# Sliding-window attention and a token-mixing MLP on one core: some transposes of x made by DMA, the mixing products with 128 columns, and a new table of emission

## The chip, the cores and the metric

The kernel runs on one core of one Trainium2 chip. The metric is the device time of one execution in microseconds (us), lower being better. A core has TensorE (PE, with its weight loads as PEld), VectorE (DVE), ScalarE (ACT), GpSimd (POOL) and SyncE (SP). Here POOL and SP only issue DMAs: POOL all loads, SP all stores.

## The reference

There are 8 batches, 8 heads, 576 tokens, and 64 channels in a head.

```python
scores = q @ k.T / 8 + slope[h] * -(i - j)      # only 0 <= i - j < 128, else -1e9
attn   = softmax(scores);  x = attn @ v          # x: (8, 576, 512), heads side by side
wq = x @ w_q;  wk = x @ w_k                      # (8, 576, 64)
mixed  = (wq @ wk.T / 8) @ x                     # token mixing; no softmax here
out    = relu(mixed) @ w_out                     # (8, 576, 512), float32
```

Because nothing stands between the two products of the mixing, the kernel computes `g = wk.T @ x` (64 x 512) first and then `mixed.T = g.T @ wq.T`.

## The kernel before, in words

All work of a batch `b` is cut into steps, each made by `plan.op(name, ...)` and belonging to one engine:

- **Loads** (POOL): q, k and v of the batch, cast to fp16 on the way (`ldsix`, `ldqk`, `ldqkt`, `ldv...`; line 234).
- **q and k transposes** (PE, then a copy by ACT or DVE out of PSUM): `tsix`, `tqk`, `tqkt` and their copies `etsix`, `etqk`, `etqkt`.
- **Scores** `sc` (line 483), exponential `exp` on ACT (L496), multiplication by the table of biases `mul` on DVE (L500). A batch has two halves `z` of two pairs of heads, and three pieces `u` in a half.
- **Values**: per pair of heads `hp` the matmuls `pva` (128-row stationary) and `pvd` (64x64 stationary), both L526; then `nrm` on DVE (L554, L555), which divides by the sums and writes x of this pair, tokens on partitions.
- **x transposed**: `xt` on PE (five transposes of 128x128, L572) into PSUM, and `ext`, a copy of 576 columns by ACT (L222) or DVE (L224) into `xT`.
- **Mixing**: `wk` (L608) and its copy `ewk`; `wq` (L637) and `ewq`; `g` (L650), whose copy into `gm` is three steps `eg` (r = None: all partitions, columns 0 to 255; r = 0 and r = 1: the halves exchanged, columns 256 to 511); then four steps `mx` (j = 0 to 3, L673), each followed by `emx`, which applies the relu and writes `rm`.
- **Output**: nine tiles of 128 tokens per pair of batches, `po` (four matmuls, L703), copy `eo`, store `st` on SP (L710).

The order of all steps is written out in the table `ORDER`. An entry is the step's number, the letter of its engine (P, A, D, G for POOL, S), for PE the PSUM bank, and `+n` for n extra matmuls on zeros (L721, `keep`) ahead of it. Each engine executes its own steps in the order of the table; semaphores between engines follow from the data and from PSUM banks. So a step whose input is late holds up everything behind it on its engine.

A mixing step uses the PE array in a tile shape: `xt`, `tqk`, `wk`, `po`, `pva` use the whole 128x128; `sc`, `pvd`, `mx` 64x64; `wq`, `g`, `tsix` 128 (or 96) rows by 64 columns.

The last PE steps of the table, from the mixing of batch 4 on (an argument is the batch, then the pair of heads, the column j, the first token of the tile, or half and piece):

```
wk(4) pvd(5,3) tqk(6,c1,x1) g(4) wq(4) xt(5,3) mx(4,j1) mx(4,j3) mx(4,j0) wk(5) tqk(6,c1,x0) mx(4,j2) g(5) sc(6,z0u1)
sc(6,z1u0) sc(6,z0u0) po(4,o384) sc(6,z0u2) po(4,o128) sc(6,z1u1) sc(6,z1u2) wq(5) tqk(7,c0,x1) po(4,o256) pva(6,1)
pva(6,0) mx(5,j0) pvd(6,1) tqk(7,c1,x1) pvd(6,0) mx(5,j1) po(4,o0) tqk(7,c0,x0) pva(6,2) mx(5,j2) pvd(6,2) mx(5,j3)
xt(6,0) tqk(7,c1,x0) pva(6,3) xt(6,2) pvd(6,3) sc(7,z0u1) sc(7,z0u0) po(5,o640) xt(6,3) po(5,o768) sc(7,z1u2)
sc(7,z0u2) po(5,o512) pva(7,0) xt(6,1) pvd(7,0) sc(7,z1u1) sc(7,z1u0) wk(6) xt(7,0) wq(6) pva(7,1) pva(7,3) pvd(7,1)
g(6) pvd(7,3) pva(7,2) xt(7,1) pvd(7,2) mx(6,j1) po(5,o1024) xt(7,3) xt(7,2) mx(6,j3) mx(6,j0) mx(6,j2) po(5,o896)
wk(7) po(6,o256) g(7) wq(7) po(6,o128) mx(7,j0) mx(7,j1) mx(7,j3) po(6,o0) mx(7,j2) po(6,o384) po(7,o512) po(7,o896)
po(7,o640) po(7,o768) po(7,o1024)
```

Of the kernel before, what the change touches and what calls it, by code (L numbers as in the profile page):

```python
# [13 lines left out]
P = 128  # L14
S = 576
D = 64
# [15 lines left out]
0G 1D 2A 4G 3D 5G 21D 31G 6D 32G 22A 20D 7D 33G 24A 34G 39G 40G 23D 12A 48P0+8 41G 14A 8A 50P1+2 42G 15A 51D 18A  # L32
43G 52P2+2 9A 16D 11A 35G 10D 17A 54P3+2 36G 49A 53D 55A 37G 64P4+3 19D 65A 38G 70P6 13D 67P0 44G 68A 66D 45G
71A 69D 46G 56P2+8 47G 73P4 72D 57A 58P3 25G 78P0 59D 74P 26G 60P6 75D 83P2 130G 61A 62P7 84A 131G 79P 132G 76P6
80D 63A 133G 77A 86P4+1 85D 89P2 138G 87A 81P7 139G 82D 90A 88D 140G 92P0+5 91D 143P6 141G 93P 144A 145P4 94D
142G 97P2 146A 98P 134G 159P6 99D 95P5 160A 135G 149P4 147P0 96D 136G 150A 100P1 148D 137G 101A 161D 162P2+2 27G
102P6 163A 28G 104P7 103D 164D 106P5 105A 29G 165P0 107A 108D 166A 30G 168P2 169P 109A 167D 231G 151P4 116P6
170D 114P0 152A 229G 153P5 115A 117D 171P4 154A 234G 155P2 172A 178P0 156D 110P6 230G 157P3 179A 173P4 158D 228G
111A 174P 112P0 180D 184P2 113A 235G 175D 232G 181P6+3 185A 121P0 233G 182A 127P1 186D 236G 122D 124P4 128A 183D
123S 176P5 129S 125A 187P2 238G 177D 243P6 126S 188P 320G 244A 192P0 189D 249P7 239G 247P4 250A 190P5 248D 193P  # L40
118P6 237G 194D 241P2 240G 119A 191D 195P3 242A 120S 318G 245P7 196D 246D 197P4 317G 251P0 198A 254P2 319G 252A
273P6 201P5 414G 255A 253D 332P4 324G 204D 199P0 274A 256D 323G 257P2 333D 202A 270P6 258A 407G 275D 271A
276P2+3 259D 322G 277A 260P6+2 272D 261P 203D 200A 265P2 278D 325G 205P4 207P0 262D 266P 206A 208A 328P4 267D
408G 326P5 329A 211P6 209P0 327D 284P2 212A 502G 330P4 210D 285P 331A 412G 263P6 286D 268P7 213P5 321G 264A 269A
287P0 405G 214A 340P2 288D 353P6 341A 215S 403G 337P4 334P0 354A 342D 225P2 409G 335A 355D 219P3 226D 338A 410G
279P6 216P0 336D 227S 220A 339D 404G 280P 221S 217A 356P4 281D 359P2 357A 218S 222P1 406G 360A 282P0 499G 358D
343P6 348P4 283D 415G 344P 361D 289P2 413G 345D 349P 290A 291P3 411G 350D 420P0 292A 293P2 416G 223D 421A 426P6
224S 294D 296A 295D 497G 428P7 427A 297P4 301P0 429D 299P2 302A 417G 346P6 300D 351P7 298A 367P0 352D 362P2 347A
419G 368P 363P 369D 303P4 422P7 418G 304A 364D 370P6 500G 311P4 371A 423D 507G 424P5 312A 305P0 589G 425D 313S
365P1 496G 306A 430P2 366D 511P6 431A 307S 498G 372P7 512D 449P4 503G 373A 432D 433P0 450A 452P2 376P6 501G 453A  # L50
374P7 451D 314P4 506G 377D 434A 454D 308P5 315D 594G 375A 379A 435D 513P2 316S 458P0 587G 309D 514A 459P 378D
310S 439P4 460D 504G 384P6 382P2 440P 385A 383D 461P0 508G 380P6 462D 386P2 381A 441D 436P0 586G 387A 509P6 437A
391P7 510D 505G 394P2 438D 392D 600G 515P3 395A 444P4 393S 516D 397P0 396S 597G 596G 536P6 398D 445P 537A 520P2
446D 595G 399S 605P1 521A 442P0 592G 606D 517P6 539P4 518A 538D 523P2 682G 447P1 522D 540A 542P6 519D 588G 543A
448D 455P4+2 541D 400P1 591G 456A 544D 526P6 401D 524A 593G 527P 457D 545P4 402S 388P1 601G 443A 528D 463P2 679G
389A 525D 546P 464P 390S 590G 547D 529P0 531P6 530A 607P1 690G 465D 532P 608A 548P4 598G 533D 466P5 603P0 599G
467A 550P2 549D 604A 534P1 468P6 602G 535D 551P 469A 684G 611P7 552D 472P5 612A 680G 470P4 473D 475A 474D 553P1
471A 683G 554A 478P2 482P6 476P4 479D 483A 555P0 686G 477D 609P1 556A 480P2 610D 559P6 687G 481D 616P4 681G 562A
632P0 617A 560D 613P2 561D 493P7 688G 633A 618D 619P4 494D 685G 614A 487P6 634D 495S 620A 635P0 689G 615D 638P2
557P7 488D 639A 691G 694P4 621D 489S 490P5 636A 640D 695D 627P2 558A 622P0 491A 637D 563P6 628P 492S 564A 698P4  # L60
629D 623P 699A 565P6 484P5 624D 566A 692P2 485A 641P0 693A 567P6 486S 642P 569P4 625P3 643D 570A 696P2 626A
646P4 697D 644P0 568A 647P 645D 703P2 648D 700P6 704A 574P1 701A 649P0 705D 577P4 575D 725P2 702D 578A 576S
706P6 571P5 726A 650D 579S 709P0 707A 727D 630P4 710P 722P2 631A 711D 719P6 723A 651P4 708D 712P0 720A 653P1
724D 714P2 652A 713D 733P6 572A 721D 715P 654A 573S 655P4 716D 734P 657A 728P0 656A 735D 717P5 658A 729P 718A
661P2 583P4 730D 662A 736P6 584A 731P7 737D 665P2 659P0 732D 585S 663P4 666A 580P6 660D 664A 738P7 581D 673P2
739A 582S 742P3 674A 740P0 675S 744D 745A 743A 670P1 741D 746P4 749P6 671A 755P2 748D 667P0 756A 757D 672S 747A
751A 752P2 750A 668D 676P1 753A 754A 669S 758P4 677A 767P5 678S 759A 761P6 760S 768D 764P7 762D 769S 770P0 763S
765A 766S 771A 772S
# [93 lines left out]
PAIRED = (2,3)  # L162
# [5 lines left out]
def kernel(  # L168
# [17 lines left out]
    on = pool.tile([P, 4 * H], F16, name="on")  # L186
    rel = pool.tile([P, 256], I32, name="rel")
# [13 lines left out]
    xs = [pool.tile([P, NT, DM], F16, name=f"x{i}") for i in range(NX)]  # L201
# [35 lines left out]
    def load_qk(b):  # L237
        t0 = (b - 2.2) * PERIOD
        if b < 2:

            n = 2
            for h in range(0, H, n):
                for x, src in ((0, q), (1, k)):
                    load("ldsix", six[x][b][:, h : h + n, :], src[b, h : h + n].rearrange("h (p j) d -> p h (j d)", j=6),
                         96 * n, 1536, (-200 if b == 0 else -170) + (0 if h < 4 else 12) + h, [("six", x, b, y) for y in range(h // 2, (h + n) // 2)], slow=1.08)
            return

        for c in range(2 if b in PAIRED else 4):
            for x, src in ((0, q), (1, k)):
                if b in PAIRED:  # L250
                    load("ldqk", nat[x][b % NN][:, c].rearrange("p (h e) -> p h e", e=128),
                         src[b, :, 256 * c : 256 * c + 256, :].rearrange("h (p j) d -> p h (j d)", j=2),
                         1024, 512, t0, [("nat", x, b % NN, c, y) for y in range(2)], reads=[("sixed", x, b % NN, y) for y in range(4)])
# [4 lines left out]
        if b % 2 == 0:  # L258
# [508 lines left out]
```

## Time and profile before

| what | value |
|---|---|
| median of 3 runs | 154.22 us (153.65 to 154.37) |
| the profiled execution | 152.65 us, of which the span is 150.9 us |
| PE busy | 136.5 us (91%) |
| DVE, ACT busy | 113.9 us, 114.0 us (76% each) |
| POOL busy (issuing loads) | 93.8 us (62%) |
| x transposes on PE | 160 matmuls, 13.9 us busy, 220 ns each |
| copies of xT | ACT 14 of 652 ns, DVE 18 of 453 ns |
| mixing products L673 | 128 matmuls, 8.3 us busy, 296 ns each |

Matmuls overlap in the array, so the busy time of a group on PE is more than what it adds; the time from the start of one step to the start of the next is the better measure, and the prediction uses it. [...] The profiled execution is one run; it was 1.57 us faster than the median.

### The profile page before, as it was taken

How to read it: one execution, taken by the hardware profiler on the slowest of the kernel's cores; microseconds unless marked ns; L12 is line 12 of the kernel's file. 1: busy time of each engine (PE TensorE's matmuls, PEld its weight loads, DVE VectorE, ACT ScalarE, POOL GpSimd, SP SyncE). 2: the span in 40 equal slices, each digit the busy share in tenths (PEclk: the TensorE clock that was granted, in tenths of full speed). 3: DMA queues.
4: the chain of work that ended last, by engine and by line, in shares of the span. 5: the costliest groups of instructions: out<-in, count | busy, mean ns of one | idle time of the engine just before them, and what ended most of it. 6: DMA issues, size and time to landing. Idle time of an engine off the chain costs nothing.

```text
span 150.9 us, 6271 instructions
## 1 busy us (share of the span) xinstructions
PE 136.5 (91%) x2755; PEld 91.7 (61%) x2755; DVE 113.9 (76%) x221; ACT 114.0 (76%) x181; POOL 93.8 (62%) x123
## 2 busy tenths in 40 slices
PE   6989999799995896999999898997799999999990
PEld 2356677565783674577676656587656776866330
DVE  7497788687659995798868979895699697995430
ACT  7956968796579789859679649955879998885831
POOL 7999997599686668994999694959880000000000
PEclk9999999999999999999999999999999999999999
DMA  2999999999999999999999999999999313013365
GB/s 29 146 148 141 150 140 147 188 163 160 212 225 204 178 155 171 171 246 174 189 176 215 178 205 187 219 207 171 143 133 195 115 74 139 17 61 150 150 269 195
DMA packets 95674, 24.64 MB, mean 163 GB/s; under 512 B 87456, under 2 KB 91040, under 8 KB 95648
## 3 DMA queue, kind: packets, MB, share of 16 engines
q0 software_dynamic: 90464, 14.82, 142.3%
q1 hardware_dynamic: 5184, 9.44, 17.8%
q8 instruction: 21, 0.34, 1.0%
q14 instruction: 5, 0.04, 0.1%
HBM read 29.62 MB, written 9.44 MB: 259 GB/s over the span
## 4 chain that ended last, share of the span: by engine, by line
PE 48%; POOL 17%; DMA 11%; ACT 9%; DVE 7%; issue 5%; DVEq 0%; POOLq 0%; ACTq 0%
PE psb L703 17%; POOL vn L234 7%; PE psb L526 7%; DMA natk<-in_k_dram 6%; ACT pt L496 6%; DMA vn<-in_v_dram 5%; PE psb L483 5%; PE psb L418 4%; PE psb L572 4%; POOL natk L234 4%; POOL natq L234 4%; PE psb L608 3%; PE psb L673 2%; DVE x L555 2%; PE psb L637 2%
## 5 line engine op out<-in xcount | busy, mean ns | idle before, releaser
L496 ACT ACTIVATE pt<-psb 128x1024 f16<-128x1024 f32 x48 | 46.6, 1031 | 4.0 <-PE psb L483 3.6
L234 POOL DMA_DIRECT2D vn<-in_v_dram x44 | 36.6, 849 | 8.2 <-PE psb L572 2.1
L500 DVE TENSOR_TENSOR pt<-pt,bt 128x1024 f16<-128x1024 f16 x48 | 32.3, 686 | 6.7 <-ACT pt L496 6.4
L703 PE MATMUL psb<-wout,rm 128*128 128x512 f16 x144 | 35.5, 380 | 0.0
L526 PE MATMUL psb<-vn,pt 64*64 64x65 f16 (+1 forms) x832 | 27.9, 194 | 1.8 <-DMA vn<-in_v_dram 0.8
L526 PEld LDWEIGHTS <-pt 64*64 64x64 f16 (+1 forms) x832 | 23.3, 103 | 7.4 <-issue 2.9
L555 DVE TENSOR_TENSOR x<-psb,inv 128x640 f16<-128x640 f32 x32 | 26.4, 824 | 1.1
L222 ACT COPY qkT<-psb 128x1024 f16<-128x1024 f16 (+1 forms) x23 | 19.6, 850 | 7.9 <-PE psb L378 4.0
L234 POOL DMA_DIRECT2D natq<-in_q_dram x28 | 23.4, 843 | 3.2 <-DMA natq<-in_q_dram 1.6
L234 POOL DMA_DIRECT2D natk<-in_k_dram x28 | 23.4, 846 | 2.9 <-DMA natq<-in_q_dram 1.4
L703 PEld LDWEIGHTS <-rm 128*128 128x128 f16 x144 | 12.2, 98 | 13.1 <-issue 0.9
L222 ACT COPY osb<-psb 128x512 f32<-128x512 f32 x21 | 12.5, 595 | 9.2 <-PE psb L703 8.7
L483 PE MATMUL psb<-qkT 64*64 64x192 f16 (+2 forms) x672 | 17.3, 228 | 2.2 <-issue 1.3
L224 DVE COPY qkT<-psb 128x1024 f16<-128x1024 f16 (+1 forms) x20 | 15.8, 788 | 4.3 <-PE psb L378 2.4
L483 PEld LDWEIGHTS <-qkT 64*64 64x64 f16 x672 | 12.1, 106 | 8.6 <-issue 6.3
L622 ACT ACTIVATE rm<-psb 128x576 f16<-128x576 f32 (+1 forms) x26 | 14.5, 599 | 2.8 <-PE psb L673 2.7
L721 PE MATMUL psb<-wz 128*128 128x512 f16 x43 | 13.6, 438 | 2.6 <-ACT pt L496 1.4
L572 PE MATMUL psb<-idn,x 128*128 128x128 f16 x160 | 13.9, 220 | 1.2 <-DVE x L555 0.9
L224 DVE COPY osb<-psb 128x512 f32<-128x512 f32 x15 | 10.3, 688 | 4.6 <-PE psb L703 4.5
L572 PEld LDWEIGHTS <-x 128*128 128x128 f16 x160 | 9.5, 98 | 4.8 <-DVE x L555 2.7
L554 DVE RECIPROCAL inv<-psb 128x10 f32<-128x10 f32 x32 | 6.9, 217 | 6.1 <-PE psb L526 4.5
L222 ACT COPY xT<-psb 128x576 f16<-128x576 f16 x14 | 9.0, 652 | 1.8 <-PE psb L572 1.7
(64 smaller groups left out, 148.7 us busy)
## 6 DMA issues: line engine op xcount, KB each, us to landing
out_dram<-osb SPq DMA_DIRECT2D x36, 256.0 KB, 4.7
vn<-in_v_dram POOLq DMA_DIRECT2D x28, 128.0 KB, 7.4
natq<-in_q_dram POOLq DMA_DIRECT2D x16, 128.0 KB, 6.4
natk<-in_k_dram POOLq DMA_DIRECT2D x16, 128.0 KB, 7.0
natq<-in_q_dram POOLq DMA_DIRECT2D x8, 144.0 KB, 5.1
natk<-in_k_dram POOLq DMA_DIRECT2D x8, 144.0 KB, 5.4
vn<-in_v_dram POOLq DMA_DIRECT2D x16, 64.0 KB, 5.3
natk<-in_k_dram POOLq DMA_DIRECT2D x4, 256.0 KB, 7.4
```

The source lines that it names most:

```text
L222: nc.scalar.copy(o, i)
L224: nc.vector.tensor_copy(out=o, in_=i)
L234: plan.op(name, {eng: issue}, lambda e: e_.dma_start(out=dst, in_=src), prio, reads=reads, writes=writes, lat=-slow * n * max(17.5, w / 21 ...
L483: nc.tensor.matmul(ps32(g)[half : half + 64, o : o + hi - lo], qkT[pb][r, i, 1, hp, k0 : k0 + 64], qkT[pb][r, i, 0, hp, q0 + lo - c : q0 + ...
L496: nc.scalar.activation(out=cols(pt, 64), in_=ps32(g).rearrange("t (a s c) -> t a s c", a=2, s=2), func=AF.Exp, scale=SCALE)
L500: nc.vector.tensor_tensor(out=cols(pt, 64), in0=cols(pt, 64), in1=cols(bt[:, z], 0), op=ALU.mult)
L526: nc.tensor.matmul(ps32(gv)[lo:hi, o : o + D + 1], pt[klo:khi, a, y, c : c + m], vv[klo:khi, kb, 2 * hp + a, :], **flags)
L555: nc.vector.tensor_tensor(out=xs[b % NX][:, :, 128 * hp : 128 * hp + 128].rearrange("t j (a d) -> t a j d", a=2), in0=px[:, :, :, 0:D], in ...
L572: nc.tensor.transpose(ps16(g)[:, 128 * t : 128 * t + 128], xs[b % NX][:, t, 128 * hp : 128 * hp + 128], idn)
L622: nc.scalar.activation(out=o, in_=s, func=AF.Relu, scale=WSCALE)
L703: nc.tensor.matmul(ps32(g), rm[pb][:, db, o : o + 128], wout[:, db, :], start=(db == 0), stop=(db == 3))
L721: nc.tensor.matmul(psb[:, g.bank, :], wz[:, 0:P], wz[:, 0:512], start=True, stop=True)
```

## The change

1. For the eleven pairs (batch, pair of heads) in `XD` (all of batches 5 and 6, the pairs 0 to 2 of batch 7) the steps `xt` and `ext` are left out. In their place stands one step `xd` on SP, a transposing DMA from `x` (128 x 640 fp16, 160 KB) straight into `xT`.
2. For that, `x` is laid out by pairs of heads (`[P, 4, NT, P]` in place of `[P, NT, DM]`), so that a pair is one contiguous row of 640. The transpose now also writes the 64 padding columns of `xT`, so the first matmul of `pvd` takes constants (`cz`) that make x of the padding tokens zero: one 64x64 matmul of 65 columns in place of another.
3. `mx` makes one product of 64 rows by 128 columns for each half of the partitions (2 matmuls of 288 columns) in place of two products of 64x64 (4 matmuls of 288).
4. `ORDER` is a new table: another order on every engine, another choice of ACT or DVE for many copies, other PSUM banks, and 44 extra matmuls in place of 43.
5. `SIX`, `QG`, `VG` are new names whose values leave the loads as they were.

```diff
+SIX = (0, 1)
+XD = ((5, 0), (5, 1), (5, 2), (5, 3), (6, 0), (6, 1), (6, 2), (6, 3), (7, 0), (7, 1), (7, 2))
+PAIRED = (2, 3)
+QG, VG = 8, 8
...
+    cz = pool.tile([P, 129], F16, name="cz")
...
-    xs = [pool.tile([P, NT, DM], F16, name=f"x{i}") for i in range(NX)]
+    xs = [pool.tile([P, 4, NT, P], F16, name=f"x{i}") for i in range(NX)]
...
+            nc.vector.memset(cz[:, 0:64], 0.0)
+            nc.vector.memset(cz[:, 64:129], 1.0)
...
                     if t == 0:
-                        mm(a, 0, 0, 64, 64, 128, 64, 64, 4, start=False, stop=False)
+                        nc.tensor.matmul(ps32(gv)[0:64, 512 * a : 512 * a + D + 1], cz[64:128, 65:129],
+                                         cz[64:128, 0:65], start=False, stop=False)
...
-                out=xs[b % NX][:, :, 128 * hp : 128 * hp + 128].rearrange("t j (a d) -> t a j d", a=2),
+                out=xs[b % NX][:, hp].rearrange("t j (a d) -> t a j d", a=2),
...
-                nc.tensor.transpose(ps16(g)[:, 128 * t : 128 * t + 128], xs[b % NX][:, t, 128 * hp : 128 * hp + 128], idn)
+                nc.tensor.transpose(ps16(g)[:, 128 * t : 128 * t + 128], xs[b % NX][:, hp, t, :], idn)
...
+        if (b, hp) in XD:
+            def xd(e, hp=hp):
+                nc.sync.dma_start_transpose(out=xT[b % NX][:, hp, 0:640].rearrange("p (t n) -> p t n", n=P),
+                                            in_=xs[b % NX][:, hp].rearrange("t j d -> t (j d)"))
+
+            plan.op("xd", {"SP": 1.0}, xd, t2, reads=[("xs", b % NX, hp)], writes=[("xT", b % NX, hp)], lat=3.0)
+            return
...
-                                     xs[bs][:, t, 256 * a : 256 * a + 256], start=(t == 0), stop=(t == NT - 1))
+                                     xs[bs][:, 2 * a : 2 * a + 2, t, :], start=(t == 0), stop=(t == NT - 1))
...
                     r = slice(64 * c, 64 * c + 64)
-                    for y in range(2):
-                        o = 256 * (j // 2 ^ c) + 128 * (j % 2) + 64 * y
-                        nc.tensor.matmul(ps32(g)[64 * y : 64 * y + 64, 512 * c : 512 * c + 288],
-                                         gm[i][r, o : o + 64], wqT[i][r, :], start=True, stop=True)
+                    o = 256 * (j // 2 ^ c) + 128 * (j % 2)
+                    nc.tensor.matmul(ps32(g)[:, 512 * c : 512 * c + 288], gm[i][r, o : o + 128], wqT[i][r, :],
+                                     start=True, stop=True)
...
-            plan.op("mx", {"PE": 0.125}, mm, tm, ps_new=[g4], mode="B", ...)
+            plan.op("mx", {"PE": 0.125}, mm, tm, ps_new=[g4], mode="D", ...)
```

The PE steps of the new table from the mixing of batch 4 on:

```
wk(4) tqkt(6) sc(5,z0u2) sc(5,z1u2) g(4) wq(4) sc(5,z1u0) pva(5,0) pvd(5,0) mx(4,j0) mx(4,j1) pva(5,3) mx(4,j2)
pvd(5,3) mx(4,j3) tqk(6,c0,x0) tqk(6,c0,x1) pva(5,2) pva(5,1) pvd(5,2) pvd(5,1) tqk(6,c1,x1) tqk(7,c0,x1) po(4,o384)
sc(6,z0u1) sc(6,z0u2) po(4,o0) sc(6,z0u0) sc(6,z1u2) po(4,o256) sc(6,z1u0) po(4,o128) sc(6,z1u1) pva(6,1) wk(5)
pvd(6,1) wq(5) g(5) pva(6,0) pvd(6,0) mx(5,j2) mx(5,j1) tqk(7,c1,x0) tqk(7,c1,x1) mx(5,j0) mx(5,j3) pva(6,3)
tqk(7,c0,x0) pva(6,2) pvd(6,3) pvd(6,2) sc(7,z1u2) po(5,o512) sc(7,z0u0) sc(7,z0u1) po(5,o768) sc(7,z0u2) sc(7,z1u1)
po(5,o1024) po(5,o640) pva(7,0) sc(7,z1u0) pvd(7,0) pva(7,1) wk(6) pvd(7,1) wq(6) g(6) pva(7,2) pva(7,3) pvd(7,2)
mx(6,j2) mx(6,j3) pvd(7,3) mx(6,j1) mx(6,j0) po(5,o896) xt(7,3) po(6,o384) po(6,o0) po(6,o256) wk(7) wq(7) g(7)
po(6,o128) mx(7,j2) mx(7,j1) mx(7,j0) mx(7,j3) pad2 po(7,o1024) po(7,o768) po(7,o512) po(7,o640) po(7,o896)
```

Two orders on other engines matter as well. The three copies `eg` come in the new table as r0 (ACT), r1 (DVE), None (ACT) for batch 5; r1 (ACT), None (ACT), r0 (DVE) for batch 6; None (ACT), r1 (DVE), r0 (DVE) for batch 7. On SP, `xd(5,1)` stands behind the store of `po(4,o384)`, `xd(6,2)` behind that of `po(5,o512)`, and `xd(7,2)` directly behind `xd(7,1)`.

More of the change, by code (lines that the diff above doesn't have):

```diff
@@ L37 @@
[L37 to L41, printed above, removed]
@@ L238, in load_qk @@
         t0 = (b - 2.2) * PERIOD
-        if b < 2:
+        if b in SIX:
             n = 2
@@ L243, in load_qk @@
                 for x, src in ((0, q), (1, k)):
-                    load("ldsix", six[x][b][:, h : h + n, :], src[b, h : h + n].rearrange("h (p j) d -> p h (j d)", j=6),
-                         96 * n, 1536, (-200 if b == 0 else -170) + (0 if h < 4 else 12) + h, [("six", x, b, y) for y in range(h // 2, (h + n) // 2)], slow=1.08)
+                    load("ldsix", six[x][b % NN][:, h : h + n, :], src[b, h : h + n].rearrange("h (p j) d -> p h (j d)", j=6),
+                         96 * n, 1536, (-200 if b == 0 else -170) + (0 if h < 4 else 12) + h if b < 2 else t0 + 0.1 * h, [("six", x, b % NN, y) for y in range(h // 2, (h + n) // 2)], slow=1.08,
+                         reads=[("sixed", x, b % NN, y) for y in range(h // 2, (h + n) // 2)] + [("natd", x, b % NN)])
             return
@@ L257, in load_qk @@
                          1024, 256, t0, [("nat", x, b % NN, c // 2, c % 2)], reads=[("sixed", x, b % NN, y) for y in range(4)])
-        if b % 2 == 0:
+        if b % 2 == 0 and (b not in SIX or b + 1 not in SIX):
             p = b // 2
@@ L278, in load_v @@
             for t in range(4):
[L279 to L280 removed]
+                for y in range(0, H, VG):
+                    load("ldv", vv[:, t, y : y + VG, 0:D], v[b, y : y + VG, 128 * t : 128 * t + 128, :].transpose([1, 0, 2]),
+                         128 * VG, 256, -164 + t if b == 1 else t0, [("vn", b % NV, t, h // 2, h % 2) for h in range(y, y + VG)])
     def setup():
```

92 lines of the change are left out of this document (47 added, 45 removed).

## The prediction

> **What bounds the kernel now.** I read the page's summary and slices, then the busy time by windows, the waits, the timeline, and SP's landing times.
>
> ```profile
> PE 136.5 (91%) x2755; PEld 91.7 (61%) x2755; DVE 113.9 (76%) x221; ACT 114.0 (76%) x181; POOL 93.8 (62%) x123
> ...
> DMA  2999999999999999999999999999999313013365
> ```
> ```profile
> 110.00:120.00 10.00, 9.98 (x207) 6.47 (x204) 9.32 (x17) 9.31 (x13) 2.52 (x3) 1.00 1.74 158
> 120.00:130.00 10.00, 9.89 (x242) 7.12 (x238) 8.11 (x15) 9.24 (x13) 0.00 (x0) 1.00 0.22 83
> ```
> From 110 us on PE (first column after the length) never pauses, while DVE, ACT and, once POOL has issued its last load at 111.6 us, the DMA engines (next to last column: 0.22) have room. To learn what each step adds, I matched the matmuls to the table, step by step, and took start to start. The timeline shows it:
>
> ```profile
> 120.82 0.45 PE L572 MATMUL psb<-idn,x 128*128 128x128 f16 x5
> 121.11 0.61 PE L418 MATMUL psb<-idn,natq 128*128 128x128 f16 x8
> ...
> 134.22 0.78 PE L572 MATMUL psb<-idn,x 128*128 128x128 f16 x10
> 134.93 0.56 PE L673 MATMUL psb<-wqT,gm 64*64 64x288 f16 x12
> 135.43 0.39 PE L703 MATMUL psb<-wout,rm 128*128 128x512 f16 x1
> ```
> One `xt` adds 0.29 us before a step of the same tile shape; two add 0.71, the last being followed by another shape. Over all steps an `xt` adds 0.279 alone and each change of shape 0.095. Likewise `po` 0.864, `pva` 0.30, `pvd` 0.20, `sc` 0.245, `tqk` 0.446, `wk` 0.588, `wq` 0.49, `g` 0.57, `mx` 0.125, an extra matmul 0.217. With 155 changes of shape the table adds up to 125.8 us; from PE's first matmul at 1.2 us to its last step the trace takes 19.8 more: 9.0 before 50 us, 9.3 from 50 to 110, only 1.5 after. So after 110 us whatever PE saves or waits shows one for one in the end; before, part of it disappears among other waits.
>
> **PE work.** Eleven `xt` go: 11 x 0.279 = -3.07. The new table has 157 changes of shape (+0.19) and one extra matmul more (+0.22). Sum -2.66. The constant matmul in `pvd` has the shape of the one it replaces: 0.
>
> **The mixing product.** Three `mx` above (12 matmuls) add 0.50 with a change of shape, so four matmuls of 288 columns take about 0.13 and must run beside each other in the four quarters of the array. Two products of 64 rows by 128 columns need the two row halves to run beside each other; no row has this shape. Bounds: 0 if they do, 32 x 0.125 = +4.0 if not. I take 0, since the four quarters contain two row halves.
>
> **Loads.** PE's waits for loads lie in batches 0 to 3:
>
> ```profile
> PEld L407 <- DMA natk<-in_k_dram: 1.0, 1, 1.0
> ...
> PE psb L526 <- DMA vn<-in_v_dram: 0.8, 1, 0.8
> ```
> Adding POOL's issues in the order of each table (0.65 to 0.89 us each) and the PE steps ahead of each load's first user gives the smallest lead for batches 1, 2, 3, 4: before -1.0, 0.9, 1.1, 2.9; after -0.7, 1.6, 2.5, 4.3. The leads grow by more than the wait at L407 lasted: -0.9 there, and -0.4 for batch 1. I take -1.3 (bounds -2 and 0).
>
> **Copies of g, the term against.** The three `eg` run one after another although two engines share them:
>
> ```profile
> 137.84 0.74 PE L650 MATMUL psb<-x,wkn 128*64 128x256 f16 x10
> ...
> 138.69 0.43 DVE L224 CAST gm<-psb 64x256 f16<-64x256 f32 x1 [1.50 <-PE psb L650]
> ...
> 139.15 0.75 ACT L222 CAST gm<-psb 64x256 f16<-64x256 f32 x2 [0.57 <-DVE gm L224]
> 139.96 0.27 PEld L673 LDWEIGHTS <-gm 64*64 64x64 f16 x12 [0.42 <-ACT gm L222]
> ```
> `g` ends at 138.58, DVE copies, ACT waits for DVE, and `mx` starts 1.38 later. Here `wq` and `po` just cover it. In the new table the first `mx` needs the last of the three copies in batches 5, 6 and 7, and the steps between are pva, pvd (0.69); pva, pva, pvd (1.00); one po (0.96). Needed from the start of the step after `g` are about 1.5. Wait: 0.8 + 0.5 + 0.55, so +1.9 in a stretch without slack (bounds 1.2 and 2.4). In batches 0 to 4 the same count gives 1.75 after, against 1.4 that the trace of before shows (0.39 in batch 2, 0.98 in batch 4): +0.3. Behind the waiting `mx` all of PE is queued, the `po` of the tail too.
>
> **The tail.** Before, `po` steps separate the last `mx` from the `po` of batch 7. After, only the two extra matmuls (in the PE sum) do, while DVE makes three relus of 0.45 first (the half-width L624, 452 ns). About 1.4 from `mx` to the first relu needed against 1.0 of cover: +0.4 (bounds 0.3 and 0.85).
>
> **Copies of x.** DVE and ACT lose eleven `ext`; that is worth only what PE waited for them. In all, 0.9 us idle stands before L608; I take -0.4 (bounds -0.9 and 0).
>
> **The transposing DMA.** No row shows one. The nearest are the stores, also issued by SP, of 256 KB against 160. Their times to landing, for those issued from 105 to 118 us and from 118 to 130 us:
>
> ```profile
> DMA to landing us min/median/max: 3.7/4.0/5.1
> ```
> ```profile
> DMA to landing us min/median/max: 2.0/2.1/2.1
> ```
> From issue to the `wk` that needs it there are, by the step sums: `xd(5,1)` 3.5 (`pvd(5,1)` to `wk(5)` 6.9, less two `nrm` of 1.04 and a copy on DVE, and the store ahead of it on SP); `xd(6,2)` 3.8; `xd(7,2)` 3.2 to 3.6. `xd(5,1)` lands beside the last loads: 4.0 by the first row, wait +0.5. The others fall after the loads, where up to 3.2 is free: 0. Bounds for landing: 2.0, the fastest store, and 8.4, the slowest of the run; a wait below zero is excluded, as the step only replaces work already taken out. The stores behind an `xd` on SP are needed by nobody but their buffers.
>
> [...]
>
> **Sum.** -2.66 + 0 - 1.3 + 1.9 + 0.3 + 0.4 - 0.4 + 0.5 = -1.3 us. The profiled execution took 152.65 (span 150.9 and 1.75 around it), so 151.35. That execution was 1.57 below the median of the runs, so I forecast 154.22 - 1.3 = **152.9 us**.
>
> **Rivals.**
> - *The transposes land late* (slower). If an `xd` takes 6.5 us among the loads (the slowest store issued from 90 to 105 us took 6.9) and 5 after them (between 2.0 and 8.4), PE waits 3.0 at `wk(5)`, 1.2 at `wk(6)`, 1.4 at `wk(7)`: 5.1 more than forecast, 158.0. It turns to slower than before once the three waits exceed 1.8, at a landing of about 5 and 4. For it: writing columns is another pattern than storing rows, and four of these fall among loads. Against it: 2.0 for 256 KB once the loads are over. Chance 0.15, its weaker forms (155 to 157) included.
> - *The two halves of `mx` run in turn* (slower): +4.0, of which about 3 show, 155.9. Against it the 0.13 of four matmuls. Chance 0.07.
> - *The copies of g don't hold PE* (faster): if they overlap, or the waits disappear in others, 1.9 + 0.3 go: 150.7. For it: they are different parts of `gm`. Against it: six waits of DVE or ACT for the other's copy of `gm` in the list of waits, 2.8 us. Chance 0.17.
> - *The change doesn't do what it says*: the transposes leave PE, but the new order loses as much in waits that I haven't counted, from PSUM banks above all; PE waited 9.3 us between 50 and 110, and 20% of that is 2: 154.9 (0.06).
>
> **Numbers.** The forecast's own case has 0.55, from 151.2 to 155.0 by the bounds of loads and copies; 0.30 of it is faster by over 0.5%, 0.18 within, 0.07 slower. A measurement can tell about 0.5% (0.77 us) from no change. Faster: 0.30 + 0.17 = 0.47. Within: 0.18. Slower: 0.07 + 0.15 + 0.07 + 0.06 = 0.35. The range takes in the fast rival and most of the slow ones: 150.2 to 156.8.
>
> **What would show it.** L572 falls from 160 to 105 matmuls, L673 from 128 to 64 of about the same 0.3 us; xT copies from 32 to 21. PE's excess over its step sum after 110 us rises from 1.5 to about 4, at the first `mx` of batches 5 to 7 and before the first `po` of batch 7; idle time before the load of `gm` names ACT or DVE. A `wk` that waits for `xT` by DMA for over 1 us in batches 6 and 7 proves the late landing; a step of `mx` near 0.25, the halves in turn. If PE's excess stays below 2, the copies were harmless and the forecast too slow.

## The result, and the profile after

The changed kernel took 161.3 us (median of 4 runs, 158.2 to 162.5), the kernel before 154.3 in the same series: a ratio of 1.036, 95% interval 1.027 to 1.044. (Ratios here leave out executions over 1.5% above the fastest of the same kernel, two of the changed kernel's four, so they are not exactly quotients of the medians.) The forecast was 152.9 with a range up to 156.8: wrong in sign and outside the range. The profiled execution took 160.33 us with a span of 158.6, so 7.7 more span than before.

The summary says that there is less work and a longer time: PE lost 118 matmuls and yet shows more busy time, since its clock was not full all the time (0.964 in the mean, 0.998 before). The slices of 4 us show where: from 108 to 128 us.

```profile
PE 138.2 (87%) x2637; PEld 90.4 (57%) x2637; DVE 105.4 (67%) x214; ACT 113.7 (72%) x179; POOL 93.8 (59%) x123
...
PEclk9999999999999999999999999998795599999998
DMA  2999999999999999999999999999999425696435
```

The same stretches as in the prediction (length; then busy time of PE, PEld, DVE, ACT, POOL; then PE's clock, the DMA share, GB/s):

```profile
110.00:120.00 10.00, 7.02 (x110) 3.23 (x108) 4.89 (x8) 6.75 (x8) 2.69 (x4) 0.84 2.09 151
120.00:130.00 10.00, 8.62 (x163) 6.93 (x163) 5.00 (x9) 3.95 (x8) 0.00 (x0) 0.67 0.68 132
```
The prediction's rows show 207 and 242 matmuls in them at full clock; now there are 110 and 163, at 0.84 and 0.67. DVE and ACT are idle too: all three wait for something else. PE's longest waits, in the list of waits, name it:

```profile
PE psb L623 <- DMA xT<-x: 4.4, 1, 4.4
PE psb L426 <- DVE x L563: 2.2, 1, 2.2
...
PE psb L534 <- DMA vn<-in_v_dram: 0.2, 1, 0.2
```
L623 is `wk`. The timeline shows the one `wk` that waits, `wk(5)`, with the clock still low behind it (20 matmuls of `wk` take 0.59 at full clock):

```profile
116.83 0.19 PE L623 MATMUL psb<-wkw,xT 128*128 128x64 f16 x1
121.38 1.19 PE L623 MATMUL psb<-wkw,xT 128*128 128x64 f16 x19 [4.35 <-DMA xT<-x]
```
The chain of waits for 105 to 128 us has the transposing DMA of the last pair of heads of batch 5, `xd(5,1)`, as its longest piece (start, length):

```profile
112.08 9.24 DMA xT<-x
```
Besides landing late it was issued late. Its input was ready at 108.8 us, but on SP it stands behind the store of `po(4,o384)`, and this store waited for its copy on ACT, which in turn stood behind the copy of `tqk(7,c0,k)`. SP's waits from 97 to 128 us have it:

```profile
SPq L724 <- ACT osb L225: 3.1, 1, 3.1
```
PE came to the tile of `wk(5)` that needs it 4.8 us after the issue, so a landing of 9.2 left a wait of 4.4. Issued when its input was ready, 3.3 us earlier, and with the same landing, it would have left an estimated 1.1. No run tries that order on SP.

The groups of `xT` on SP for the four transposes of batch 5 (102 to 114 us) and for the next two (114 to 128 us) give the duration on SP in ns and the time to landing:

```profile
L603 SPq DMA_TRANSPOSE xT<-x x4: 1302/1408/1458, 103.2 to 112.1; - x4
...
DMA to landing us min/median/max: 8.6/9.1/9.5
```
```profile
L603 SPq DMA_TRANSPOSE xT<-x x2: 1200/1204/1207, 124.3 to 127.9; - x2
...
DMA to landing us min/median/max: 2.6/2.6/2.6
```
One and the same DMA lands after 2.6 us when no loads run and after 9 when they do. What runs beside it suffers as well. To see this without the change of order, the measure is experiment 3 below, which has the new order and all loads but no such DMA before 121 us. Two lines on landing after the change: the stores issued between 105 and 118 us (experiment 3: 2.7 to 5.2; before: 3.7/4.0/5.1), then the loads of v issued between 97 and 113 us (before: 6.1/6.7/7.0):

```profile
DMA to landing us min/median/max: 6.4/7.2/7.9
```
```profile
DMA to landing us min/median/max: 8.7/11.2/13.6
```
Of these nine loads the last five, issued from 108 us on, land after 11.2 to 13.6 us, and after 5.8 to 6.5 in experiment 3. The first four, issued from 97 to 100 us, take 8.7 to 10.5, and 9.8 to 10.8 in experiment 3: those are slow without the transposes too.

Matching matmuls to the table as the prediction did, PE's time beyond its step sums is 30.4 us against 19.8. Up to 100 us it fell by 0.45; from 100 us on it rose from 4.1 to 15.1. With 2.66 less work this makes 11.0 - 0.45 - 2.66 = +7.9, and the span grew by 7.7. The 11.0 are, in the main: `wk(5)` 5.0; a gap ahead of `tqk(7,c0,k)` at 106.4 us, 2.4 where before had one of 1.0 (+1.4; it is the wait at L426 above, which the list puts down to DVE; experiments 7 and 10 show another cause); `po(4)` at half clock behind that gap, 1.15; five steps at half clock behind `wk(5)`, 1.85; the copies of g and the tail, 1.9. These add to 11.3; the other steps lose 0.3 less than before.

### The profile page after: what moved, and what is told of

It reads as the page before. It is cut to its first block, busy times and chain, and to the rows that moved or that the text cites. A ratio compares the mean times of both kernels' runs of the same rounds, so it can differ in the third digit from the quotient of the medians.

```text
span 158.6 us, 6048 instructions
## 1 busy us (share of the span) xinstructions
PE 138.2 (87%) x2637; PEld 90.4 (57%) x2637; DVE 105.4 (67%) x214; ACT 113.7 (72%) x179; POOL 93.8 (59%) x123
## 4 chain that ended last, share of the span: by engine, by line
PE 52%; DVE 16%; ACT 14%; DMA 9%; issue 5%; POOL 1%; SPq 0%; ACTq 0%; POOLq 0%; DVEq 0%
PE psb L717 15%; PE psb L534 7%; ACT pt L504 7%; DMA xT<-x 6%; DVE x L563 6%; PE psb L491 5%; PE psb L735 3%; DMA natk<-in_k_dram 3%; PE psb L426 3%; PE psb L415 3%; PE psb L580 3%; DVE gm L227 3%; DVE qkT L227 3%; DVE pt L508 2%; PE psb L623 2%
## 5 line engine op out<-in xcount | busy, mean ns | idle before, releaser
L717 PE MATMUL psb<-wout,rm 128*128 128x512 f16 x144 | 36.3, 390 | 0.2
L225 ACT COPY qkT<-psb 128x576 f16<-128x576 f16 (+1 forms) x27 | 21.8, 823 | 8.5 <-PE psb L426 3.6
L563 DVE TENSOR_TENSOR x<-psb,inv 128x640 f16<-128x640 f32 x32 | 26.4, 825 | 1.1
L534 PEld LDWEIGHTS <-pt 64*64 64x64 f16 (+1 forms) x768 | 22.7, 105 | 5.5 <-issue 3.0
L491 PE MATMUL psb<-qkT 64*64 64x192 f16 (+2 forms) x672 | 18.0, 233 | 2.1 <-issue 1.8
L225 ACT COPY osb<-psb 128x512 f32<-128x512 f32 x20 | 11.8, 591 | 9.2 <-PE psb L717 9.2
L637 ACT ACTIVATE rm<-psb 128x576 f16<-128x576 f32 (+1 forms) x28 | 15.4, 618 | 4.2 <-PE psb L687 4.2
L227 DVE COPY qkT<-psb 128x1024 f16<-128x1024 f16 (+1 forms) x16 | 11.4, 727 | 4.3 <-PE psb L386 1.3
L623 PE MATMUL psb<-wkw,xT 128*128 128x64 f16 x160 | 6.7, 199 | 4.4 <-DMA xT<-x 4.4
L580 PE MATMUL psb<-idn,x 128*128 128x128 f16 x105 | 9.2, 220 | 0.8 <-DVE x L563 0.6
L687 PE MATMUL psb<-wqT,gm 64*128 64x288 f16 x64 | 7.9, 288 | 2.0 <-DVE gm L227 0.6
```

Of the source, the lines that this page charges most:

```text
L225: nc.scalar.copy(o, i)
L227: nc.vector.tensor_copy(out=o, in_=i)
L491: nc.tensor.matmul(ps32(g)[half : half + 64, o : o + hi - lo], qkT[pb][r, i, 1, hp, k0 : k0 + 64], qkT[pb][r, i, 0, hp, q0 + lo - c : q0 + ...
L534: nc.tensor.matmul(ps32(gv)[lo:hi, o : o + D + 1], pt[klo:khi, a, y, c : c + m], vv[klo:khi, kb, 2 * hp + a, :], **flags)
L563: nc.vector.tensor_tensor(out=xs[b % NX][:, hp].rearrange("t j (a d) -> t a j d", a=2), in0=px[:, :, :, 0:D], in1=inv[iv].unsqueeze(3).bro ...
L580: nc.tensor.transpose(ps16(g)[:, 128 * t : 128 * t + 128], xs[b % NX][:, hp, t, :], idn)
```

## Experiments

Three theories. **A**: the four transposes of batch 5 and the loads beside them slow each other; PE waits at `wk(5)`, and the clock drops behind the gaps. **B**: the new order loses by waits of its own, whatever the DMAs do. **C**: the two halves of the new mixing product run in turn. In the diffs a table entry is told by the name of its step.

**1. The code alone, with the old table.**

```diff
-XD = ((5, 0), (5, 1), ..., (7, 1), (7, 2))
+XD = ()                          # all x by xt and ext
-ORDER = new table
+ORDER = table of before
```


> The old order of steps, all x transposes on PE, but the rest of the change's code: mixing products with 128 columns, x laid out by pairs of heads, the constant matmul. Theory A (the four transposing DMAs of batch 5 land late because they run beside loads; PE stands still 4.5 us at wk(5), and its clock halves afterwards) expects no effect: 154.3 us within 0.8. Theory B (the new order of steps loses by itself) expects the same. Theory C (the two products of 64 rows and 128 columns don't run beside each other) expects up to +4, some 157 to 158 us, and an mx step of 0.25 us.

Measured: 153.4 us, 0.991 (0.985 to 0.997). C is out: with 64 products of the new shape the kernel is, if anything, a little faster. In the profile after, the group of L687 has 64 matmuls with a mean of 288 ns, where before had 128 of 296.

**2. The old table with the transposes by DMA that come after the loads.**

```diff
-XD = ((5, 0), (5, 1), ..., (7, 1), (7, 2))
+XD = ((6, 0), (6, 1), (6, 2), (6, 3), (7, 0), (7, 1))
-ORDER = new table
+ORDER = table of before, each xt and ext of these replaced by xd behind its nrm
```


> The old order of steps, with the transposing DMA for batch 6 and the pairs 0 and 1 of batch 7 alone, each right behind its nrm; these start after the last load has been issued. Theory A: they land in 2.6 to 3 us, where 5 us and more are free, so 6 xt are saved on PE, 6 x 0.28 = 1.7 us: 152.6 us, clock 0.998. A rival (any transposing DMA costs PE more than it saves, loads or not) expects 154.3 or more.

Measured: 153.95 us, 1.002 (0.994 to 1.009). They land after 2.6 to 4.8 us and hold nobody up. But the 6 x 0.279 = 1.7 us of PE work that is gone can't be seen in the time either: beside experiment 1, the same code and order with all transposes on PE, the kernel is if anything slower. Why stays open.

**3. and 4. The new table, with batch 5 on PE, and with all of x on PE.** I put the steps `xt` and `ext` where PSUM banks were free.

```diff
-XD = ((5, 0), ..., (5, 3), (6, 0), ..., (7, 2))
+XD = ((6, 0), ..., (7, 2))       # 3
+XD = ()                          # 4
+ORDER: xt(5,hp), ext(5,hp) (4: all eleven) ahead of their wk
```


> The changed kernel with the x transposes of batch 5 back on PE (xt and ext put into free PSUM banks of the new order); seven transposing DMAs stay. Theory A: the wait of 4.5 us at wk(5), the slower clock after it (about 2.5 us), the longer gap at 106 us (1.5) and the slower clock after that (1.7) go, four xt of 0.28 to 0.37 come back: 160.3 - 10.2 + 1.3, about 151.5 us of the profiled kind, 151 to 153; loads of batch 7 land in 6 to 7 us again instead of 9 to 13.6. Theory B: stays at 156 or more.

> The new order of steps with all x transposes on PE. Theory A: as the run without batch 5's, plus seven xt of 0.28 to 0.37 (2.2 us): 153 to 155 us. Theory B: 157 or more, that is, slow without a single transposing DMA.

Measured: 157.9 us, 1.022 (0.9995 to 1.044), and 160.9 us, 1.042 (1.024 to 1.060). Read plainly this is B. But the traces show losses that my placing made. In number 3, `tqk(6)` and the inserted `xt` wait for each other's copies out of PSUM banks, 0.4 us at most in one place, and the steps there lose some 1.4 in all. In number 4 such waits are 0.9, 0.7 and 0.4, and it has 11 x 0.28 us more work. The new order has its `nrm` so close to `wk(5)` that four `xt` fall into the scores of batch 6, where ACT has six exponentials of 1.03 us to make and DVE six multiplications of 0.69. The longest waits of number 3 from 100 us on are others, though: two of 1.3 us in which PE waits for nothing that the profile shows (experiments 7 and 8 show what they are), and one for a late transpose at `wk(6)`, with three stores beside it:

```profile
PE psb L532 <- issue: 2.6, 2, 1.3
...
PE psb L621 <- DMA xT<-x: 0.8, 1, 0.8
```
So these two don't separate A from B, and the next four were made to. How much the new order loses with all loads and no transposes beside them, no run measures cleanly.

**5. and 6. Fewer loads, in the new kernel and in the old one.** The late loads fetch one head of eight: v of batches 6 and 7, and five of the eight loads of q and k of batch 7. The work on PE, ACT and DVE is the same as with all loads; the rest of these loads is left out.

```diff
+        few = slice(0, 1) if b in (6, 7) else slice(0, H)
-            load("ldv", vv[:, t, y : y + VG, 0:D], v[b, y : y + VG, ...
+            load("ldv", vv[:, t, few, 0:D], v[b, few, ...
+ ldvt, and ldqk of batch 7 with c >= 2 or (c, x) = (0, q), in the same way
```


> The changed kernel as it is, but the loads that are under way beside the transposes of batch 5 are cut: v of batches 6 and 7, and four of the eight wide q/k loads of batch 7, fetch one of the eight heads (the other heads hold what an earlier batch left there). Theory A (the four transposes of batch 5 land late because the loads beside them hold the DMA engines, PE waits 4.5 us, its clock drops): the four land after 2.6 to 4 us, the wait at wk(5) is under 0.5 us, PE has no gap over 2 us there, time 151 to 154 us. Theory B (the new order loses by waits of its own, whatever the DMAs do): the wait at wk(5) goes as well, but 157 us or more stays, with the excess spread over 40 to 60, 80 to 100 and 120 to 150 us. Between the two, 154 to 157: both have a share.

> The same loads cut in the kernel before: what the cut is worth without transposes by DMA. Before shows 0.5 us of excess a 10 us stretch beside these loads, so both theories expect 153.5 to 154.5 us, ratio 0.995 to 1.002. If it gains over 1 us, the gain of e5 must be read against this run and not against before.

Measured: the new kernel 151.8 us, 0.981 (0.963 to 0.999); the old one 153.7 us, 0.998 (0.990 to 1.006). The whole loss of the new kernel is gone. By the medians it is 1.9 us ahead of the old one with the same loads, but the intervals of the two ratios overlap, so that lead isn't settled. The four transposes of batch 5 in the new kernel with fewer loads:

```profile
L603 SPq DMA_TRANSPOSE xT<-x x4: 1199/1280/1978, 104.6 to 111.3; - x4
...
DMA to landing us min/median/max: 2.6/3.2/4.9
```
`wk(5)` doesn't wait, and PE's waits from 98 to 128 us, in full, are 0.9, 0.3 and 0.3 us:

```profile
PE psb L534 <- issue: 0.9, 1, 0.9
PE psb L687 <- ACT gm L223: 0.3, 1, 0.3
PE psb L687 <- ACT rm L637: 0.3, 1, 0.3
```
The span is 150.0 us, 8.6 under that of the changed kernel, and the time beyond the step sums 21.9 in place of 30.4 (8.5). As it was worded B falls: with the same order and the same steps only the loads' bytes differ. But fewer loads also take the gap of 2.4 us at 106.4 away, and that one, as the next experiments show, is not of the transposes' making. So what falls is a loss by the order alone; a loss by the order together with the loads stays in.

**7. and 8. Transposes that nobody waits for, and plain copies of the same bytes,** in the kernel of experiment 1.

```diff
+        if b == 5:                # after each nrm(5,hp), on SP
+            def extra(e, hp=hp):  # 7
+                nc.sync.dma_start_transpose(out=scr[:, hp].rearrange("p (t n) -> p t n", n=P),
+                                            in_=xs[b % NX][:, hp].rearrange("t j d -> t (j d)"))
+            def extra(e, hp=hp):  # 8
+                nc.sync.dma_start(out=scr[:, hp], in_=xs[b % NX][:, hp].rearrange("t j d -> t (j d)"))
```


> Old table, new code, all x still transposed by PE; after each of the four normalisations of batch 5, SP also transposes x by DMA into a tile that nothing reads. Theory A (the transposes and the loads slow each other): the transposes land after 7 to 10 us, the loads issued beside them after 8 to 13 us in place of 6 to 7, and as no matmul waits for the transposes, the time stays within 1 us of the run with the code alone (153.4), unless a late load or a late fetch of PE's instructions costs 1 to 3 us; such a cost would show as a gap in PE at the positions of the code fetches or behind a tile of batch 6. Theory B: the DMAs do nothing to the time, and the transposes land after 2.6 to 5 us.

> The same as the run with the unread transposes, but with plain copies of the same 40 KB a pair of heads, SBUF to SBUF. If it is the bytes or the number of DMAs that hurt, landings and time are as with the transposes. If it is the transposing (256-byte packets, and 1.2 us of SP each), the copies land after 3.5 to 6.5 us as the stores do, the loads beside them after 6 to 8 us, and the time is that of the run with the code alone, 153.4.

(The four DMAs move 160 KB each; the 40 KB in the expectation was a slip.) Measured: with transposes 155.4 us, 1.012 (0.998 to 1.026); with copies 151.3 us, 0.987 (0.976 to 0.998); without either (experiment 1) 0.991. The first can't be told from before, but it can from the other two. The landing of the four DMAs, transposes first:

```profile
DMA to landing us min/median/max: 7.0/9.3/10.2
```
```profile
DMA to landing us min/median/max: 4.2/5.0/5.8
```
The loads of v beside them (issued between 97 and 113 us) landed after 7.7 to 12.1 us beside transposes, after 5.0 to 6.3 beside copies, and after 4.3 to 5.5 in experiment 1. So it isn't the 160 KB and not the number of DMAs. It may be the packets: the four transposes move 2,560 of 256 bytes, the four copies 512 of 1,280, and a copy in pieces of 256 bytes wasn't run. The whole times of the two profiled executions (156.96 and 156.28 us) don't tell them apart, since the one with copies lost time before 60 us. What counts is PE's time beyond the step sums from 110 to 120 us: 4.1 us with transposes, 1.0 with copies, 0.5 in experiment 1. Of the 4.1, 2.3 are one gap in which PE waits for nothing that the profile shows, between two matmuls of one step; the clock is at half for 3.4 us behind it:

```profile
114.00 0.42 PE L491 MATMUL psb<-qkT 64*64 64x64 f16 x13
116.51 0.74 PE L491 MATMUL psb<-qkT 64*64 64x192 f16 x15 [2.09 <-issue]
```
It stands at PE's instruction number 4289 (all records of PE in order of start: matmuls, weight loads and a few on semaphores), and 4289 = 16 x 256 + 193. In the 14 traces of this case, packets of 16,384 bytes on the queue that the view of DMA calls q8, instruction, go with the numbers that leave 193 when divided by 256. Where PE stands still at such a number for 0.9 us or more and no load or copy came late, it goes on 1.2 to 1.6 us after the packet has landed (1.9 once, in experiment 13). I read it as the next 256 instructions, come late: before, 21 such packets go with 5,523 records of PE, after the change 20 with 5,288. The packet starts some time after PE has passed the place 256 instructions earlier; this time differs with what else the DMA engines have to do:

| kernel | number | passing to packet, us | packet, us | gap, us |
|---|---|---|---|---|
| before | 4033 | 3.5 | 0.9 | 0.96 |
| after | 4033 | 4.5 | 1.6 | 2.42 |
| new order, batch 5 on PE (3, 4, 11) | 4033 | 4.8, 4.4, 4.5 | 1.4, 1.6, 1.5 | 1.47, 1.03, 1.09 |
| new order, few loads (5) | 4033 | 1.3 | 1.0 | 0.05 |
| before | 4289 | 2.8 | 1.5 | none |
| code alone (1), with copies (8) | 4289 | 0.8, 1.7 | 0.9, 1.1 | none |
| with transposes (7) | 4289 | 6.3 | 1.2 | 2.34 |
| after | 4289 | 5.5 | 1.7 | none (PE waits at `wk(5)`) |

So beside loads alone a fetch waits up to 4.8 us in this table (4.9 at number 1729 after the change), with transposes beside them 5.5 and 6.3. The clearest comparison is number 4289 in one and the same order: 0.8 with neither, 1.7 with copies, 6.3 with transposes. The gap of 2.4 at number 4033 in the changed kernel comes soon after the first transposes are issued (103.2 us), and its fetch is no later than in the new order without them; there PE has more to do in between. So this gap is put down to the loads and the order, the one of experiment 7 to the transposes. (The list of waits names DVE's L563 for the former in the changed kernel; in experiment 10 PE goes on 0.2 us before the step of DVE that would have released it is over, and after the change the PSUM bank that the step writes had been freed at 105.4 us, a microsecond before the gap.)

**9. The chain of batch 5 later,** with all transposes and loads as in the changed kernel.

```diff
 ORDER, PE's steps from pva(6,1) on
-pva(6,1) wk(5) pvd(6,1) wq(5) g(5) pva(6,0) pvd(6,0) mx(5,j2) ...
+pva(6,1) pvd(6,1) pva(6,0) pvd(6,0) tqk(7,c1,q) tqk(7,c1,k) tqk(7,c0,q) pva(6,3) pva(6,2) pvd(6,3) pvd(6,2)
+sc(7,z1u2) wk(5) sc(7,z0u0) wq(5) sc(7,z0u1) g(5) sc(7,z0u2) mx(5,j2) mx(5,j1) mx(5,j0) mx(5,j3) sc(7,z1u1) ...
```


> The changed kernel with one stretch of its table in another order: wk, wq, g and mx of batch 5 come about 4 us of PE work later, behind pv of batch 6, the last transposes of q and k of batch 7 and the first scores of batch 7; all transposes by DMA and all loads stay. Theory A (the late landing of batch 5's transposes is the wait that costs): wk(5) waits under 1 us though the transposes still land after 8 to 10 us; PE's half-clock stretch behind that wait goes; 152.5 to 156 us. What stays of the loss is the gap in PE near 106 us (2.4 us before) with its half-clock stretch. Against A: 158 us or more with wk(5) not waiting.

Measured: 163.5 us, 1.054 (1.043 to 1.066): a miss. `wk(5)` no longer waits for `xT` (the four still land after 8.4 to 9.4 us). But the chain now stands among the scores of batch 7, where ACT has its exponentials of 1.03 us to make. The copies of g and the relus queue behind them, and the four `mx`, which take 0.5 us when nothing holds them, spread over 2.9. PE's time beyond the step sums between 120 and 140 us is 9.0 in place of 2.7.

```profile
128.85 0.29 PE L685 MATMUL psb<-wqT,gm 64*128 64x288 f16 x1 [0.45 <-ACT gm L223]
...
129.71 0.42 PE L685 MATMUL psb<-wqT,gm 64*128 64x288 f16 x3 [0.56 <-ACT gm L223]
...
130.63 0.30 PE L685 MATMUL psb<-wqT,gm 64*128 64x288 f16 x2 [0.51 <-ACT pt L502]
```

**10. Work for PE while it waits.**

```diff
 ORDER
-wk(5) on bank 3
+wk(5) on bank 3, +20             # 20 matmuls on zeros ahead of it
```


> The changed kernel with 20 more matmuls on zeros (0.217 us each, 4.3 us) just ahead of wk(5), so that PE works while it waits for the transposes. It tells the wait itself from the slow clock that follows it: by Theory A the work after wk(5) then runs at full clock, where 6.8 us at half clock cost about 3.4 us: 157 to 159 us, mean granted clock 0.975 or more. If the clock part is nothing, 161 us.

Measured: 160.0 us, 1.037 (1.027 to 1.047), the same as the changed kernel. The clock does what was expected; from 121 to 127 us, first the changed kernel, then this one:

```profile
121.00:127.00 6.00, 5.62 (x84) 4.33 (x85) 2.26 (x5) 1.60 (x5) 0.00 (x0) 0.54 0.78 146
```
```profile
121.00:127.00 6.00, 5.51 (x98) 3.73 (x97) 2.59 (x6) 1.96 (x5) 0.00 (x0) 1.00 0.84 184
```
The 157 to 159 us that I expected did not come: the median is 1.3 us lower, the ratio isn't. In the traces, the stretch from the end of `wk(5)` to the last `tqk` of batch 7 is 1.2 us shorter than in the changed kernel, while a wait of 0.5 for a copy of g comes back. So of the 1.85 listed above for the half clock behind `wk(5)` no more than 1.3 is won, and these runs can't tell it from nothing; the wait itself is what costs.

In the changed kernel's trace the clock was at half for 6.8 us from 119.7 us on, at `wk(5)`, where PE idled 4.4 us; it fell as well at 109.4 us, for 3.4, behind a gap of only 2.4.

**11. The order of 9, with batch 5 on PE,** so that no transpose by DMA is issued beside the loads.

```diff
-XD = ((5, 0), ..., (5, 3), (6, 0), ..., (7, 2))
+XD = ((6, 0), ..., (7, 2))
 ORDER of experiment 9
+xt(5,0) behind pva(6,1), xt(5,3) behind pvd(6,1), xt(5,2) and xt(5,1) around tqk(7,c1,q); ext on ACT
```


> As the run with the chain later, but the four x of batch 5 are transposed by PE (copied out by ACT), the seven others by DMA; so no transposing DMA is issued beside the loads. PE has 4 x 0.28 us more to do than in the run with few loads (151.8 us). Theory A: loads land after 6 to 7 us, no PE gap over 1.5 us between 100 and 125 us, 151.5 to 154 us, under the run with batch 5 on PE in its earlier places (157.9). Theory B (the new order loses by itself, whoever transposes): 156 us or more.

Measured: 163.1 us, 1.051 (1.037 to 1.065): a miss in time. Its first half holds: the loads issued from 109 us on land after 5.8 to 7.1 us. The gap at number 4033 is 1.09. But the stretch from 125 to 135 us has the same waits as in experiment 9, so it is the order of 9 that is bad, with or without transposes by DMA. These two say nothing against A, and give no better kernel.

**12. and 13. The loads behind the transposes, all data loaded.** A copy of one column on POOL reads a landed `xT`, and POOL's later loads queue behind it.

```diff
+            if b == 5 and hp in (1,):     # 12;  13: (1, 2)
+                def gate(e, hp=hp):
+                    nc.gpsimd.tensor_copy(out=gt[:, hp : hp + 1], in_=xT[b % NX][:, hp, 639:640])
 ORDER, POOL
+gate(5,2)                                 # 13 only
 ldqk(7,c2,k) ldqk(7,c3,q) ldqk(7,c2,q) ldqk(7,c3,k) ldqk(7,c0,q)
+gate(5,1)
 ldv(7,t1) ldv(7,t0) ldvt(7) ldv(7,t2) ldv(7,t3)
```


> The changed kernel, complete, with the five loads of v of batch 7 held back on POOL until the last transpose of batch 5 has landed (a one-column copy on POOL reads it), so 5 of the 16 loads that ran beside the transposes start behind them. PE needs v of batch 7 some 13 us later. Theory A: the last of the four transposes lands after 3 to 6 us in place of 9.2, wk(5) waits 0 to 2 us in place of 4.5, its half-clock stretch shrinks or goes, the loads held back land after 6 to 9 us; 154.5 to 158 us. If the transposes are slow for a cause of their own, whatever loads run, wk(5) still waits over 3 us and the time is 160 us or more.

> As the run before, and the last five loads of q and k of batch 7 wait until the third transpose of batch 5 has landed, so only loads of v of batch 6 and earlier ones run beside the first three. Theory A: all four transposes land after 2.6 to 6 us, wk(5) does not wait, the gap of PE at its instruction fetch near 106 us is nearer 1.0 us (before) than 2.4; the time falls to 151.5 to 156 us, unless q and k of batch 7, now landing near 120 us, make PE wait in turn; then the wait stands at the transposes of batch 7's q and k (tqk), near 122 us. Against A: 158 us or more with no such wait.

Measured: 158.3 us, 1.025 (1.015 to 1.034), and 159.4 us, 1.034 (1.023 to 1.045). In 12 the v loads start later, but 11 others still run: the transposes land after 8.1 to 9.8 us, the last after 8.3 (I had expected 3 to 6), and `wk(5)` waits 3.2. In 13 the four land after

```profile
DMA to landing us min/median/max: 3.6/4.7/5.5
```
and `wk(5)` waits 0.2. The loss moves with the overlap, though: the three transposes issued from 117.8 to 126.5 us, now beside the loads held back, land after 5.8 to 11.5 us, and PE waits for the late loads:

```profile
PE psb L425 <- DMA natq<-in_q_dram: 1.6, 1, 1.6
...
PE psb L533 <- DMA vn<-in_v_dram: 1.1, 1, 1.1
```
This confirms it with all data loaded: the transposes get quick as soon as the loads are out of their way, and the loads and transposes that meet instead get slow. A kernel with the new order that neither cuts loads nor lets them meet a transpose was not found. So the 151.8 us of experiment 5 is what the order takes with the collision and most of the late loads taken away, not a time of a complete kernel. Of the complete kernels the code with the old table (1) is the better one, by 0.9%; the 0.987 of number 8, which only adds copies to it, lies within its interval.

## Why the prediction was wrong, point by point

- **The transposing DMA: the step that failed.** It was sized by the stores: landing 4.0 us among loads, wait +0.5. It took 8.6 to 9.5 us, and the wait was 4.4. The bounds were 2.0 and 8.4, "the slowest store of the run"; the measured value lies beyond the upper one. Behind the step stood my assumption, which no run had shown, that any DMA issued by SP lands as its neighbours do. Experiments 7 and 8 show that this nearly holds for a copy (4.2 to 5.8) and not for a transpose (7.0 to 10.2). That the landing is what made the wait is shown by experiments 5 and 13: with landings of at most 4.9 and 5.5 us, `wk(5)` waits 0 and 0.2. The path was off as well, to the good: 4.8 us from issue to need in place of 3.5, though SP held the issue back for 3.3.
- **The rival "the transposes land late"** named the mechanism, at a chance of 0.15. Its 158.0 came from 6.5 us among loads and 5 us after them. The first was too little, the second too much: after the loads it is 2.6 us in the median and 3.7 at most, and `wk(6)` and `wk(7)` don't wait for it. That was not certain: in experiment 3 one landed after 4.4 beside stores, and `wk(6)` waited 0.8.
- **What neither case had:** that the transposes slow the loads and stores in flight. The last loads of v take 13.1 us in the median, 6.3 in the same order without transposes beside them, and the stores 7.2 in place of 4.0. Experiment 7 shows the slower loads, and an instruction fetch made late, with no wait for a transpose anywhere.
- **What the sum had no term for:** the instruction fetch among loads. At number 4033 it costs the changed kernel 1.4 us more than the one before, with 1.15 of half clock behind it. That much of B may be right: the new order seems to lose something together with the loads, also with no transposes beside them. The gaps are 1.5 us at two such numbers (3777 and 4033) in experiment 3, 1.0 at one in experiment 4 and before, and there are none at these two in experiment 1; that is too little to settle its size.
- **SP's time.** The sum has no term for it. An `xd` took SP 1.20 us alone and 1.30 to 1.46 among loads, a store 0.33. So it was not the time of SP's issuing that made the 9 us.
- **PE work, -2.66, and the mixing product, 0:** right. The matmuls of `xt` fell to 105, those of the mixing product to 64 of 288 ns, and two products of a run start 0.13 us apart, as before.
- **Loads, -1.3:** right in kind, but most of it was lost again. Up to 100 us PE's time beyond its steps fell by 0.45 in all. PE's own waits for loads fell by more than forecast, from 1.9 (the 0.8 and 0.7 below and 0.4 for `natq` at L378) to 0.2 us. What ate the gain is again the instruction fetch: its gaps (releaser "issue") grew from 1.3 to 2.7. From the list of PE's waits up to 100 us, before and after:

```profile
PE psb L483 <- issue: 1.3, 1, 1.3
...
PE psb L526 <- DMA vn<-in_v_dram: 0.8, 1, 0.8
...
PE psb L407 <- DMA natk<-in_k_dram: 0.7, 1, 0.7
```
```profile
PE psb L491 <- issue: 1.8, 1, 1.8
...
PE psb L415 <- issue: 0.9, 1, 0.9
...
PE psb L534 <- DMA vn<-in_v_dram: 0.2, 1, 0.2
```
- **Copies of g, +1.9, and the tail, +0.4:** right in kind, and near in size with some luck. Two copies on ACT, one on DVE, in turn, and `mx(6)` behind the last:

```profile
138.84 0.75 ACT L225 CAST gm<-psb 64x256 f16<-64x256 f32 x2
...
139.62 0.43 DVE L227 CAST gm<-psb 64x256 f16<-64x256 f32 x1 [0.34 <-ACT gm L225]
...
140.10 0.11 PEld L687 LDWEIGHTS <-gm 64*128 64x128 f16 x4 [0.33 <-DVE gm L227]
```
In experiment 5, where nothing else disturbs them, the first `mx` of batches 5, 6 and 7 wait 0.5, 0.4 and 0.5: 1.4, where the sum had 1.85. A later `mx(6)` waits 0.4 for a relu, which the sum didn't have, and the tail 0.6 in place of 0.4, so the total is 2.4 against 2.25 by errors that cancel. The +0.3 of batches 0 to 4 and the -0.4 for the copies of x are isolated by no run.
- **The sum without the collision** was fair as far as it can be seen: -1.3 was forecast. Experiment 5 stands 1.9 us below experiment 6 in the median, with intervals that overlap, and 0.9 below before in span. But experiment 5 also lacks what the loads do to instruction fetches, so it is no clean measure of the sum. The wait of 4.4 at `wk(5)` alone is more than the whole gain forecast; the gap at number 4033 and the half clock come on top.

## What to carry to other kernels

A DMA's time to land is taken from a DMA of the same kind in the same company: a plain store is no measure for a transpose (the stores of this stretch landed after 4.0 us in the median before the change, the transposes that came to stand there after 9.1), and a transpose with no loads beside it (2.6 us) none for one among loads of 256-byte rows (9.1). When work moves from a busy engine to the DMA engines, price it twice: what the moved transfer takes there, and what it does to the transfers that were there already, the instruction fetches among them (the last loads of v took 13.1 us in place of 6.3; with the transposes of experiment 7 the fetch for number 4289 started 6.3 us after the passing in place of 0.8). Here 3.07 us of PE work was bought with one wait of 4.4 us alone, while the seven transposes of the same kernel that were issued after the loads held nobody up. And where a DMA stands in order behind a store on the same engine, the time to price runs from the moment its input is ready: here 3.3 of the 12.6 us from there to the landing were spent behind a store that waited for its own copy.

## What the runs showed of the hardware that was not expected

- A DMA transpose of 128 x 640 fp16 from SBUF to SBUF lands after 2.6 us alone, after up to 4.8 beside a few stores or last loads (experiment 2), and after 7.0 to 10.2 beside many loads with rows of 256 bytes in DRAM (128 in SBUF); beside those held back in experiment 13 it was 5.8 to 11.5. The last five loads of v issued beside them then take 11.2 to 13.6 us (after the change), where the same loads in the same order took 5.8 to 6.5 (experiment 3). From 109 to 112 us the loads moved 0.13 MB in the changed kernel, 0.37 in experiment 3 and 0.40 before.
- The transpose's own packets are of 256 bytes and take 18 ns in the median when alone, 31 ns beside the loads, single ones up to 1.3 us (after the change).
- PE's instructions come, as I read the traces, in fetches of 256, packets of 16,384 bytes that the view of DMA counts with the others, and where such a packet came late PE stood still, 2.4 us at number 4033 after the change and 2.3 at 4289 in experiment 7: beside loads the packet starts up to 4.9 us after PE has passed the place 256 earlier, beside loads and transposes up to 6.3, and where the pause was of 0.9 us or more PE went on 1.2 to 1.6 us after the packet had landed (1.9 once).
- PE's clock fell to half behind gaps of 2.4 us (after the change, at 109.4 us) and 2.3 (experiment 7, at 116.4), not only behind the one of 4.4.
